# New places for the buffers of a convolution's backward pass (one core, tiles of 128 partitions)

## The chip, the cores and the metric

One core of one Trainium2 chip. The metric is the device time of one execution in microseconds (us). Each kernel below was run several times; I quote the median, and compare only executions whose state was told to be fast, which here is all of them. A run of a kernel also left one execution taken by the hardware profiler: its *profile*. Engines: PE is TensorE (PEld its weight loads), DVE VectorE, ACT ScalarE, POOL GpSimd.

## The reference

The program computes a network of four residual steps and all its gradients:

```python
x = A_q
x = x + A(layernorm(x), k, v, shift_k, ssm_k, ssm_D)   # gated long convolution by FFT
x = x + MLP(layernorm(x), w1, b1, w2, b2)              # gelu
x = x + A(layernorm(x), ...)
x = x + MLP(layernorm(x), ...)
# outputs: x, and the gradients of q, k, v, shift_k, ssm_k (= h), ssm_D, w1, b1, w2, b2
# S = 2048 positions, D = 512 channels, MLP width 1376, bfloat16
# A: k_shift[t] = sum of 4 taps of k times shift_k;  kv = k_shift * v
#    y = causal convolution of kv with ssm_k, + kv * ssm_D;   out = q * y
```

What matters here is the backward pass of A, which comes last: the gradient of kv leads to the gradients of v, k and of the four taps (`shift_k`), and a transform of the spectra gives the gradient of `ssm_k`, called h below.

## The kernel before

The last quarter of the program is `conv_backward`. Its parts, in program order, with cuts marked:

```python
def conv_backward(...):
    dma = nc.gpsimd.dma_start                     # all these loads and stores queue on POOL
    psum = ... "cb_ps" ...                        # "sp": two buffers of PSUM
    gyp = ... "cb_gy" ...                         # GY0..4 (spectra); "Sg": two buffers of 8 KB per partition
    # ... forward transform, products with H and KV, inverse transform into W ... (cut)
    with tc.tile_pool(name="cb_w", side="right", reuse_waits="tile") as wp:
        W = [wp.tile([P, 2, 8, 512], BF16, name=f"Wb{m}") for m in range(2)]
        # ... (cut)
        with tc.tile_pool(name="cb_io", side="right", reuse_waits="tile") as io:
            wdiag = io.tile([P, ND, 4, P], BF16, name="wdiag_b")
            ksbs = [io.tile([P, 4, D], BF16, name="ksb_b", tag="ksb", bufs=4) for i in range(4)]
            # ... loads of wdiag, ks, v (cut)
            gT = io.tile([P, ND, S + 16], BF16, name="gksT")
            nc.vector.memset(gT[:, :, S:S + 16], 0.0)
            for i in range(4):
                for h in range(4):
                    # products on VectorE; four matmuls turn gkv into PSUM tile ps (gt_ps) (cut)
                    if h >= 2:                    # and once more, reversed, into pr (gr_ps)
                        for cc in range(ND):
                            c0 = 256 * (i % 2) + P * (h - 2)
                            nc.scalar.activation(out=W[1][:, cc // 2, 2 * (cc % 2) + i // 2, c0:c0 + P],
                                                 in_=pr[:, 0, cc * P:(cc + 1) * P], func=ACT.Identity)
                    nc.scalar.activation(out=gT[:, :, t0:t0 + P], in_=ps..., func=ACT.Identity)
                yield 3.0
            w0f = W[0][:, :, :, :].rearrange("p e s d -> p (e s d)")
            kcs = [gyp.tile([P, 4096], BF16, name="kTc", tag="Sg", bufs=2)[:, 0:4 * 544] for cc in range(2)]
            kcs += [w0f[:, 2048 + 2176 * x:2048 + 2176 * (x + 1)] for x in range(2)]
            for cc in range(ND):
                dma(out=kcs[cc], in_=dram.kT[:, cc, :, :]...)
            # gradient of k: 256 matmuls gk_ps<-gksT,wdiag, evicted into gk_o (the ksb buffers), stored (cut)
            gwo = io.tile([P, 2, ND, 4], F32, name="gwo", tag="gwo", bufs=1)
            junk = W[0][:, 0, 0:2, :]...
            for cc in range(ND):                  # the shift-filter sums: 4 x 4 x 2 = 32
                for j in range(4):
                    for half in range(2):         # half 0 reads gT, half 1 the reversed copies in W[1]
                        nc.vector.scalar_tensor_tensor(out=junk, in0=g_, scalar=1.0, in1=kc[:, :, k_:k_ + 256],
                                                       op0=ALU.mult, op1=ALU.mult, accum_out=gwo[...])
                    yield 2.2
            gwb = ...; tt(out=gwb, in0=gwo[:, 0], in1=gwo[:, 1], op=ALU.add)
    # cb_io and cb_w end here; the next pool is laid over the same bytes
    with tc.tile_pool(name="cb_gh", side="right", reuse_waits="tile") as hp:      # the h gradient
        tabG = hp.tile([P, 2, 16, NQP], BF16, name="tabG")            # NQP = 272
        # ... two loads of tabG (cut)
        w0 = hp.tile([P, 2, 8, NQP], BF16, name="Wh", tag="Wh", bufs=2)
        th0 = [hp.tile([P, 2, 2, NQP], BF16, name=f"ibh{x}", tag=f"ibh{x}", bufs=3) for x in range(3)]
        gh0 = hp.tile([P, S], BF16, name="gh", tag="gh", bufs=4)
        for cc in range(ND):                      # four channel blocks
            # matmuls gh_ps<-tabG,GY; ScalarE evicts them into Wh (L871); VectorE folds Wh into gh; store (cut)
```

Each `yield N` lets another generator put in some N us of its own work, the weight gradients of the MLP (dw_tp, dw_tm, dw_ps, b1a). Tiles are placed from fixed stacks; a pool opened after another has closed takes the same bytes. `reuse_waits="tile"` means that the first write to a tile waits for all uses of every older tile whose bytes it touches, whole tiles at a time.

## Time and profile before

| | before |
|---|---|
| time, median of 3 executions | 955.77 us (954.72 to 958.27) |
| span of the profiled execution | 952.4 us |
| the changed stage within it: from gksT's memset to b_ps | 782.06 to 947.45 = 165.39 us |

The *stage* is my own measure, used throughout: from the start of VectorE's memset of gksT's pad to the start of b_ps, TensorE's last product. Everything that the change touches lies in it, but for two loads that the changed kernel issues 26.1 and 7.7 us before it. It is worth having because executions differ by some us in work that the change does not touch: over all profiles below the memset falls between 781.7 and 787.2 us, though the program up to there is practically the same, while the stage took 151.00 and 151.01 us in the two profiles of the changed kernel.

The prediction below shows the lines for the wait itself. Beside them, from the page of the kernel before: the span, the granted TensorE clock in 40 slices (tenths of full speed), and the chain that ended last, by engine.

```profile
span 952.4 us, 12919 instructions
...
PEclk9999999978998789869999999979999999997999
...
PE 37%; DVE 30%; ACT 17%; DMA 6%; issue 6%; POOL 3%; SPq 1%; ACTq 0%; DVEq 0%; POOLq 0%
```

Slice 37 of 40 (857 to 881 us) has a clock of 7 amid nines: the gap that the change aims at. VectorE has 30% of the chain, though the page gives TensorE more busy time (83% against 77% of the span). Two stretches around that gap in the kernel before (columns: stretch and length; busy us of PE, PEld, DVE, ACT and POOL with instruction counts; clock; DMA share; GB/s):

```profile
859.00:873.00 14.00, 2.25 (x22) 1.63 (x20) 13.65 (x20) 1.83 (x3) 0.00 (x0) 0.67 0.30 84
873.00:881.00 8.00, 8.00 (x52) 5.96 (x51) 6.94 (x9) 3.89 (x10) 0.78 (x1) 0.73 0.22 66
```

In the first TensorE is busy 2.25 of 14 us. In the second it is busy all the time, at 0.73 of its clock.

### The profile page before, as it was taken

To read this page: it belongs to the slowest core of one execution; us is meant where nothing else is said; L and a number is where in the kernel's file an instruction comes from. 1 tells how busy PE (TensorE), PEld (TensorE's weight loads), DVE (VectorE), ACT (ScalarE), POOL (GpSimd) and SP (SyncE) were. 2 spreads that over 40 slices of the span, in tenths; PEclk is the share of its full clock that TensorE was granted. 3 is DMA by queue.
4 is the path that set the end of the run, shared out by engine and by line. 5 is a ranking of instruction groups with operands and counts; after the bars stand their busy time and mean duration, and the time that the engine had idled before them with its cause. 6 is when DMAs were issued, how large, how long until landed. Compare 5 with 4: busy or idle time off the path is not lost.

```text
span 952.4 us, 12919 instructions
## 1 busy us (share of the span) xinstructions
PE 794.6 (83%) x4754; PEld 406.6 (43%) x4754; DVE 734.0 (77%) x1203; ACT 613.5 (64%) x810; POOL 151.7 (16%) x274
## 2 busy tenths in 40 slices
PE   3698868846786869649999999968999997995998
PEld 2463324422332324214444444434455555853664
DVE  7748489895999979658458878883389995699973
ACT  5867645637997979579835656445665558652664
POOL 5632210021001010100001221220011304200000
PEclk9999999978998789869999999979999999997999
DMA  6568786223445344476798868549076798852331
GB/s 218 173 237 322 280 286 222 90 50 105 138 150 146 130 140 148 139 215 180 249 283 241 246 190 239 166 151 353 2 244 203 266 323 287 288 170 72 118 100 38
DMA packets 157079, 180.87 MB, mean 190 GB/s; under 512 B 50325, under 2 KB 137048, under 8 KB 156504
## 3 DMA queue, kind: packets, MB, share of 16 engines
q1 hardware_dynamic: 142872, 135.70, 46.1%
q0 software_dynamic: 11968, 40.15, 11.7%
q10 hardware_dynamic: 2176, 4.19, 1.2%
q8 instruction: 37, 0.61, 0.3%
q14 instruction: 26, 0.21, 0.1%
HBM read 95.76 MB, written 82.13 MB: 187 GB/s over the span
## 4 chain that ended last, share of the span: by engine, by line
PE 37%; DVE 30%; ACT 17%; DMA 6%; issue 6%; POOL 3%; SPq 1%; ACTq 0%; DVEq 0%; POOLq 0%
PE gn_ps L1134 7%; PE sp_ps L55 7%; PE gh_ps L1116 6%; DVE Wb L55 6%; PE dw_ps L55 6%; ACT g_z L1089 3%; PE gh_ps L55 3%; DVE b1a L55 3%; ACT g_s L1065 3%; ACT g_o L1066 2%; ACT g_q L1062 2%; DVE pr_t L55 2%; DVE pr_u L55 2%; PE z_ps L1087 2%; DMA tabFb<-tabF_d 2%
## 5 line engine op out<-in xcount | busy, mean ns | idle before, releaser
L55 PE MATMUL dw_ps<-G,dw_tm 128*128 128x512 bf16 x704 | 170.8, 381 | 2.2 <-ACT dw_tm L1236 2.2
L1236 ACT ACTIVATE dw_tm<-dw_tp 128x1024 bf16<-128x1024 bf16 x88 | 89.9, 1024 | 68.2 <-PE dw_tp L55 68.2
L1087 PE MATMUL z_ps<-nT_sl,w_sb 128*128 128x512 bf16 x352 | 93.8, 424 | 32.3 <-DMA nT_sl<-n_sl 27.2
L1099 PE MATMUL o_ps<-w_sb,h_sl 128*128 128x512 bf16 x352 | 92.1, 404 | 26.7 <-DVE h_sl L1069 26.4
L55 PEld LDWEIGHTS <-dw_tm 128*128 128x128 bf16 x704 | 64.9, 98 | 62.5 <-ACT dw_tm L1236 2.9
L1118 ACT ACTIVATE gz_sl<-gh_ps 128x512 bf16<-128x512 f32 x88 | 50.2, 594 | 56.5 <-PE gh_ps L1116 53.3
L1134 PE MATMUL gn_ps<-w1T_sb,gz_sl 128*128 128x512 bf16 x352 | 81.4, 379 | 1.3 <-DVE gz_sl L1119 1.3
L1116 PE MATMUL gh_ps<-gT_sl,w2T_sb 128*128 128x512 bf16 x352 | 79.6, 379 | 0.0
L1087 PEld LDWEIGHTS <-w_sb 128*128 128x128 bf16 x352 | 37.3, 107 | 88.4 <-issue 43.0
L1089 ACT ACTIVATE g_z<-z_ps,b1col 128x512 bf16<-128x512 f32 x88 | 55.2, 708 | 27.6 <-PE z_ps L1087 27.6
L1099 PEld LDWEIGHTS <-h_sl 128*128 128x128 bf16 x352 | 35.1, 103 | 79.0 <-DVE h_sl L1069 35.3
L55 PEld LDWEIGHTS <-dw_fm 128*128 128x128 bf16 x704 | 47.8, 100 | 20.9 <-issue 0.8
L55 PE MATMUL dw_tp<-ident,dw_fm 128*128 128x128 bf16 x704 | 54.8, 222 | 0.0
L1134 PEld LDWEIGHTS <-gz_sl 128*128 128x128 bf16 x352 | 34.3, 98 | 43.2 <-DVE gz_sl L1119 2.3
L1116 PEld LDWEIGHTS <-w2T_sb 128*128 128x128 bf16 x352 | 34.4, 98 | 41.1
L55 DVE TENSOR_REDUCE b1a<-dw_fm 128x1 f32<-128x2048 bf16 x22 | 49.6, 2277 | 0.0
L989 POOL TENSOR_SCALAR rstd<-ln_mv 128x4 f32<-128x4 f32 x16 | 7.6, 475 | 248.1 <-DVE ln_mv L987 161.9
L1146 POOL TENSOR_SCALAR bb_diag<-ident,bb_cols 128x128 bf16<-128x128 bf16 x32 | 21.6, 676 | 157.3 <-DVE bb_junk L1143 148.1
L1065 ACT ACTIVATE g_s<-g_t 128x2048 bf16<-128x2048 bf16 (+1 forms) x24 | 42.8, 1784 | 3.6 <-DVE g_t L1064 3.6
L1119 DVE TENSOR_TENSOR gz_sl<-gz_sl,gpb 128x2048 bf16<-128x2048 bf16 (+1 forms) x24 | 27.2, 1134 | 22.7 <-DMA gpb<-gp_d 11.7
L1062 ACT ACTIVATE g_q<-g_z 128x2048 bf16<-128x2048 bf16 (+1 forms) x24 | 43.1, 1798 | 0.1
L1066 ACT ACTIVATE g_o<-g_t 128x2048 bf16<-128x2048 bf16 (+1 forms) x24 | 42.7, 1780 | 0.0
(297 smaller groups left out, 1621.6 us busy)
## 6 DMA issues: line engine op xcount, KB each, us to landing
dw_fm<-h_d SPq DMA_DIRECT2D x22, 512.0 KB, 3.9
dw_fm<-gz_d SPq DMA_DIRECT2D x22, 512.0 KB, 3.8
h_d<-h_sl SPq DMA_DIRECT2D x16, 512.0 KB, 2.9
gp_d<-g_p SPq DMA_DIRECT2D x16, 512.0 KB, 3.3
nb_sl<-n_d SPq DMA_DIRECT2D x16, 512.0 KB, 5.3
gpb<-gp_d SPq DMA_DIRECT2D x16, 512.0 KB, 4.5
gz_d<-gz_sl SPq DMA_DIRECT2D x16, 512.0 KB, 5.2
n_d<-n_sl SPq DMA_DIRECT2D x12, 512.0 KB, 3.3
```

What stands on the lines that cost most here:

```text
L55: return self.tc.keep_in_program_order(f(*args, **kwargs))
L1062: nc.scalar.activation(out=q, in_=zb, func=ACT.Square)
L1065: nc.scalar.activation(out=sg, in_=t, func=ACT.Sigmoid)
L1066: nc.scalar.activation(out=o, in_=t, func=ACT.Sigmoid, scale=-1.0)
L1087: nc.tensor.matmul(ps, lhsT=w.w1[:, dc, c * P:(c + 1) * P], rhs=nT[:, dc, :], start=(dc == 0), stop=(dc == ND - 1))
L1089: nc.scalar.activation(out=zb[:, c - c0, :], in_=ps, func=ACT.Identity, bias=w.b1col[:, c:c + 1])
L1099: nc.tensor.matmul(ps, lhsT=h[:, c, t * P:(t + 1) * P], rhs=w.w2[:, c, :], start=False, stop=(c == NFC - 1))
L1116: nc.tensor.matmul(ps, lhsT=w.w2T[:, dc, c * P:(c + 1) * P], rhs=gT[:, dc, :], start=(dc == 0), stop=(dc == ND - 1))
L1118: nc.scalar.activation(out=gz[:, c, :], in_=ps, func=ACT.Identity)
L1119: nc.vector.tensor_tensor(out=gz[:, c0:c0 + k, :], in0=gz[:, c0:c0 + k, :], in1=gp[:, 0:k, :], op=ALU.mult)
L1134: nc.tensor.matmul(ps, lhsT=gz[:, c, t * P:(t + 1) * P], rhs=w.w1T[:, c, :], start=(c == 0), stop=(c == NFC - 1))
L1236: nc.scalar.activation(out=dst, in_=ps, func=ACT.Identity)
```

## The change

Its intent: the first tiles that the h gradient needs (Wh, tabG) are to lie over memory that the shift-filter sums do not read. The pools of that part share one region of bytes, so this takes two things. What the sums read and lies in W has to leave W: the reversed copies and two of the kT blocks go to `gy_bf`, a tile free by then, and to a small new tile; the junk output goes there too. And the tiles are declared in another order: gksT, the one large tile that the sums read to their end, comes to lie under gh (the tile of the finished h gradient), which VectorE writes only after the sums in any case. As the reversed copies are now contiguous in a way that one instruction can write, four evictions of 128x128 become one of 128x512.

Bytes of each partition, from the programs as built:

| tile | before | after |
|---|---|---|
| gksT (read by the sums) | 81600–98112 | 56768–73280 |
| wdiag, ksb | 61120–81600 | 77760–98240 |
| first Wh | 77600–86304: on gksT | 96160–104864: on the last ksb and W[0] |
| tabG | 60192–77600: on wdiag, ksb | 113568–130976: on W |
| gh, ibh | 95008–130976 | 60192–96160: gh on gksT, ibh on kTc3, wdiag, ksb |

The diff, cut to its core:

```diff
         with tc.tile_pool(name="cb_io", bufs=1, side="right", reuse_waits="tile") as io:
+            gT = io.tile([P, ND, S + 16], BF16, name="gksT")
+            gwo = io.tile([P, 2, ND, 4], F32, name="gwo")
+            kc3 = io.tile([P, 4 * 544], BF16, name="kTc3")
             wdiag = io.tile([P, ND, 4, P], BF16, name="wdiag_b")
... (ksb)
-            gT = io.tile([P, ND, S + 16], BF16, name="gksT")
+            tf = res.gy_bf[:, :, :].rearrange("p t d -> p (t d)")
+            gr = tf[:, 0:4096].rearrange("p (c i q) -> p c i q", c=ND, i=4)
...
-                        for cc in range(ND):
-                            c0 = 256 * (i % 2) + P * (h - 2)
-                            nc.scalar.activation(out=W[1][:, cc // 2, 2 * (cc % 2) + i // 2, c0:c0 + P],
-                                                 in_=pr[:, 0, cc * P:(cc + 1) * P], func=ACT.Identity)
+                        nc.scalar.activation(out=gr[:, :, i, P * (h - 2):P * (h - 1)],
+                                             in_=pr[:, 0, :].rearrange("p (c t) -> p c t", c=ND), func=ACT.Identity)
...
-            kcs += [w0f[:, 2048 + 2176 * x:2048 + 2176 * (x + 1)] for x in range(2)]
+            kcs += [tf[:, 4096:4096 + 2176], kc3]
...
-            gwo = io.tile([P, 2, ND, 4], F32, name="gwo", tag="gwo", bufs=1)
-            junk = W[0][:, 0, 0:2, :].rearrange("p a (b d) -> p (a b) d", b=2)
+            junk = tf[:, 6272:6272 + 1024].rearrange("p (i q) -> p i q", i=4)
... (the sums read gr[:, cc] instead of W[1])
     with tc.tile_pool(name="cb_gh", bufs=1, side="right", reuse_waits="tile") as hp:
+        gh0 = hp.tile([P, S], BF16, name="gh", tag="gh", bufs=4)
+        th0 = [hp.tile([P, 2, 2, NQP], BF16, name=f"ibh{x}", tag=f"ibh{x}", bufs=3) for x in range(3)]
+        w0 = hp.tile([P, 2, 8, NQP], BF16, name="Wh", tag="Wh", bufs=2)
         tabG = hp.tile([P, 2, 16, NQP], BF16, name="tabG")
... (loads of tabG)
-        w0 = hp.tile([P, 2, 8, NQP], BF16, name="Wh", tag="Wh", bufs=2)
-        th0 = [hp.tile([P, 2, 2, NQP], BF16, name=f"ibh{x}", tag=f"ibh{x}", bufs=3) for x in range(3)]
-        gh0 = hp.tile([P, S], BF16, name="gh", tag="gh", bufs=4)
```

More of the change, by code (lines that the diff above doesn't have):

```diff
@@ L804, in conv_backward @@
                                     eng=nc.gpsimd)
-            w0f = W[0][:, :, :, :].rearrange("p e s d -> p (e s d)")
             kcs = [gyp.tile([P, 4096], BF16, name="kTc", tag="Sg", bufs=2)[:, 0:4 * 544] for cc in range(2)]
-            kcs += [w0f[:, 2048 + 2176 * x:2048 + 2176 * (x + 1)] for x in range(2)]
+            kcs += [tf[:, 4096:4096 + 2176], kc3]
             for cc in range(ND):
@@ L830, in conv_backward @@
                         else:
-                            g_ = W[1][:, cc // 2, 2 * (cc % 2):2 * (cc % 2) + 2, :].rearrange("p a (b q) -> p (a b) q", b=2)
+                            g_ = gr[:, cc]
                             k_ = 272 + j
```

## The prediction

> **What bounds the kernel now.** I read the page first, then the chain that ended last, in order of time, for the last quarter; then the waits and the timelines of single engines there. The change touches only this last quarter: the convolution's backward pass, with the MLP's weight gradients (dw_ps, dw_tp, b1a) filled in between. The chain there:
>
> ```profile
> 799.04 0.71 POOL o3B_d L244
> ...
> 802.30 15.68 DMA kTc<-kT_d
> 818.08 1.24 DVE Wb L55 x2
> ...
> 870.88 1.24 DVE Wb L55 x2
> 872.20 0.61 ACT Wh L871
> 872.85 7.65 PE gh_ps L55 x48
> ...
> 942.56 4.98 PE dw_ps L55 x23
> 947.56 0.61 ACT dw_o L1292
> ```
>
> Columns: start, length, engine and tile. From 818 to 873 us VectorE makes the 32 shift-filter sums ("Wb" is their junk output), with a b1a sum in between each few. Then one ScalarE copy of PSUM (Wh) starts, and from there TensorE sets the end. The hand-over is odd, as the h gradient (gh_ps, Wh) takes no data from the sums. The waits from 775 us on name it:
>
> ```profile
> PE gh_ps L55 <- ACT Wh L871: 12.6, 4, 11.8
> ACT Wh L871 <- DVE Wb L55: 11.4, 1, 11.4
> ```
>
> (total us, times, longest.) Each has one long wait. TensorE's timeline shows the place, and beside it the same point of the second channel block, which is undisturbed:
>
> ```profile
> 860.28 0.82 PE L55 MATMUL gh_ps<-tabG,GY 128*128 128x257 bf16 x6
> 872.85 7.65 PE L55 MATMUL gh_ps<-tabG,GY 128*128 128x257 bf16 x48 [11.75 <-ACT Wh L871]
> ...
> 887.42 0.82 PE L55 MATMUL gh_ps<-tabG,GY 128*128 128x257 bf16 x6
> 888.49 5.51 PE L55 MATMUL gh_ps<-tabG,GY 128*128 128x257 bf16 x48 [0.25 <-ACT Wh L871]
> ```
>
> TensorE fills its two PSUM buffers, then idles 11.75 us until ScalarE empties one. The sums wrote no PSUM and no Wh: the wait is one of memory. In the program as built, the first Wh tile has bytes 77600 to 86304 of each partition and gksT 81600 to 98112, so Wh may be written only when the last sum that reads gksT is over (870.88 + 1.22 = 872.1 us, and Wh starts at 872.20). Elsewhere TensorE hardly stands still: from 826 to 860 us it was busy all 34.00 us, from 881 to 948 us for 65.87 of 67. Two things about the idle time matter for its price:
>
> ```profile
> 861.00:872.80 11.80, 0.10 (x1) 0.00 (x0) 11.49 (x18) 0.60 (x2) 0.00 (x0) 0.61 0.27 78
> 872.80:876.00 3.20, 3.15 (x15) 2.21 (x15) 3.20 (x5) 1.09 (x3) 0.04 (x1) 0.50 0.00 0
> 876.00:880.50 4.50, 4.50 (x36) 3.65 (x34) 3.94 (x5) 2.54 (x6) 0.73 (x1) 0.85 0.40 117
> 888.00:894.00 6.00, 5.75 (x52) 4.84 (x50) 5.50 (x6) 4.07 (x9) 0.00 (x0) 1.00 0.54 179
> ```
>
> (stretch and length; busy us of PE, PEld, DVE, ACT, POOL; granted TensorE clock; DMA share; GB/s.) After the idle stretch the clock is 0.50 and then 0.85, later 1.00 again. And VectorE's end:
>
> ```profile
> 936.35 0.17 DVE L55 TENSOR_TENSOR b1o<-b1a 128x11 bf16<-128x11 f32 x1
> 947.71 0.21 DVE L55 COPY b1r<-b_ps 11x128 bf16<-11x128 bf16 x1 [11.19 <-PE b_ps L55]
> ```
>
> VectorE is done 11.19 us before TensorE reaches its last product: that is its slack.
>
> [...]0.50 for the 3.2 us after the gap, 1.00 for 826 to 860 us. So the gap costs more than its length. [...]while Wh waited, nothing behind it ran on ScalarE from 860.80 to 872.20 us, and no weight-gradient matmul filled TensorE's gap. [...]kTc, issued at 802.30 us behind the 1 MB copy of o1B (issued 800.64, 15.9 us to landing, so 816.5), came at 818.0. I use this for when the sums can start.
>
> **The change, part by part.** The order of instructions on TensorE, VectorE and SyncE is unchanged between the two builds, apart from names. ScalarE loses 24 instructions; on the GpSimd queue two of the four kT loads move ahead.
>
> Removed wait: the first Wh tile now has bytes 96160 to 104864, over the last ksb buffer and the start of W[0]. Its first write no longer waits for VectorE, only for its matmuls and for the second gk_o store (issued 819.76 us; the median landing is 8.5 us, so about 829). tabG now lies over W, free when the last gr_ps matmul is done (808 us). gksT's place goes to the gh tiles, which VectorE writes after the sums anyway. TensorE's wait then shrinks from 11.75 to the 0.25 us of the other blocks: **11.5 us**.
>
> Removed cold clock: the 48 matmuls took 7.65 us here and 5.51 us in block two: **2.1 us**. [...]both terms move the end in full.
>
> ScalarE's reversed copies: 8 times four copies (about 0.280 us each alone, 0.78 us as a group of four in the timeline) become 8 single ones of 128x512. I price those as the gksT copies of that size, 0.598 us. TensorE waits for the first of each pair (0.29 us four times in the timeline), so some 0.14 us shorter four times: **0.6 us**. The second copy of each pair ends before anything waits.
>
> Unchanged: the 32 sums (1.22 us each, also with junk and operand in gy_bf), all matmuls, the tail behind TensorE's last product (947.5 to 952.4 us). The kT loads for blocks three and four go out after ksb instead of at 806 us, but the sums start with block one, which still needs the buffers of vb and stands behind o1B in the queue. I leave the sums at 818 to 873 us.
>
> Sum: 11.5 + 2.1 + 0.6 = 14.2 us, so a span of 938.2 us, and 955.8 - 14.2 = **941.6 us** (1.5% less).
>
> Does VectorE have room? After the sums and two b1a (877.8 us) it works a block and its b1a in turn. In these blocks it waited 1.17, 1.10, 1.08, 1.29 and 2.15 us for Wh, together 6.8; with TensorE ahead these go. Then b1o comes at 936.4 - 6.8 = 929.6 us, TensorE's last product at 947.5 - 14.2 = 933.3: 3.7 us of slack left. Block three of gh needs the first Wh buffer again: ScalarE at 901.3 - 14.2 = 887.1 us, VectorE finished with it at 886.9 - 1.2 = 885.7. Close, 1.4 us. The dw_fm loads wait for b1a of four units earlier: the nearest, released at 877.8 us, lands at 882 and is wanted past 890.
>
> **The rivals.** (a) VectorE becomes the bound. For: only 3.7 us and 1.4 us are left, and a later start of the sums shifts all of it. Against: the five waits that go. If its times stayed as they were (b1o at 936.4), the end would come 3 us later than I say: 945 us. (b) The moved loads disturb. For: the gy_bf load can start at about 774 us, when its memory is free, and from 775 to 786 us the DMA share was 1.06 at 363 GB/s with the reloads of G. 544 KB at that rate is 1.5 us, which could hold TensorE at G or push the stores, o1B and kTc behind it: 943 us, up to 945 together with (a). (c) A new memory wait takes the old one's place, of Wh for a store or of tabG for W. Against: those are free at 829 and 808 us, 30 us before use; I see no such wait in the build. It would give back most: 950 to 956 us. (d) Less DMA behind 806 us lets kTc land earlier and the sums start sooner. That only adds to VectorE's slack and leaves 941 us; to pass 2% (936.7 us), TensorE would have to lose 5 us more, nearly all its waiting of 786 to 811 us (25.00 - 19.76 = 5.2 us), which nothing here touches.
>
> **Range and chances.** The first two terms are one gap and its cold clock, read off directly, so their error is below 1 us. (a) and (b) can take 1 to 4 us; the three runs of before lie within 3.6 us. So 937.5 to 946.5 us. Over 2% faster needs 19.1 us: 0.05. Slower by 2% has no mechanism: 0.01. Within 2%: 0.94.
>
> **What would show it.** Right: no wait of Wh for VectorE; the first 48 gh_ps matmuls in about 5.5 us with the clock at 1.00 between 860 and 880 us; TensorE's last product near 933 us; VectorE's wait for it down from 11.2 to about 4 us; the reversed copies at 0.6 us each, eight of them. Wrong: a new wait over 2 us of gh_ps for Wh in block three or four, or of dw_ps for G near 780 us (a, b); b1o after 933 us (a); or an eviction that waits for a store (c).

## The result, and the profile after

The changed kernel takes **942.22 us** (median of four, 940.49 to 943.36) against 955.44 us (four: the three above and one more; 954.72 to 958.27), with a ratio of 0.9855 [0.9829, 0.988]. That is 1.5% less, within the 2% that count as the same. Ratios and intervals here and below come with each run's result and are worked out from the fast executions, so they are not quite the ratio of the medians that I quote. The result was correct, and all executions were fast.

The profile after, the same three lines of its page:

```profile
span 940.2 us, 12816 instructions
...
PEclk9998998977999779878999999989999999999999
...
PE 52%; ACT 18%; DVE 15%; issue 6%; DMA 5%; POOL 3%; SPq 1%; ACTq 0%; POOLq 0%; DVEq 0%
```

The dip of the clock in slice 37 is gone, and the 32 sums (with the b1a between them), which had been on the chain from 818 to 872 us, are not on it any more. That VectorE's share of the chain fell as far as from 30% to 15% is only in part due to this: followed back from its new end, the chain also takes another way through the work before 800 us, which is practically the same in both kernels (from 700 to 800 us VectorE has 84 us of it before and none after, TensorE 9 and 95 us). The chain in order of time shows TensorE in their place, in the profile after (start, length, engine and tile):

```profile
858.67 1.94 PE dw_ps L55 x9
...
861.50 0.56 PE gh_ps L55 x5
862.08 0.61 ACT Wh L871
862.74 5.50 PE gh_ps L55 x48
```

The same two stretches in the profile after; this execution ran 2.1 us later at the memset, which does not matter for stretches of this length:

```profile
859.00:873.00 14.00, 13.64 (x111) 9.70 (x112) 13.76 (x19) 8.92 (x16) 0.00 (x0) 1.00 0.30 85
873.00:881.00 8.00, 7.69 (x67) 6.09 (x66) 7.87 (x10) 5.56 (x12) 0.78 (x1) 1.00 0.23 72
```

TensorE is busy 13.64 us instead of 2.25, at full clock in both. TensorE's timeline and the waits of the stage after the change:

```profile
862.74 5.50 PE L55 MATMUL gh_ps<-tabG,GY 128*128 128x257 bf16 x48 [0.25 <-ACT Wh L871]
```

```profile
DVE gy_bf L55 <- DMA kTc<-kT_d: 18.8, 1, 18.8
...
ACT Wh L871 <- PE gh_ps L55: 4.9, 14, 0.6
DVE b1r L55 <- PE b_ps L55: 4.1, 1, 4.1
...
PE gh_ps L55 <- ACT Wh L871: 1.1, 4, 0.3
```

The wait of 11.75 us is now 0.25, like the other three blocks. For Wh, ScalarE now waits only for the matmuls that it evicts (at most 0.6 us each), and not for VectorE. The first line is the wait of the sums for their first kT block, as long as before (18.9 there): nothing is changed in when the sums start, only in who waits for them. (Before, the junk output lay in Wb, so the sums were listed under Wb; now they are under gy_bf.) VectorE's end, after:

```profile
931.16 0.17 DVE L55 TENSOR_TENSOR b1o<-b1a 128x11 bf16<-128x11 f32 x1
935.46 0.21 DVE L55 COPY b1r<-b_ps 11x128 bf16<-11x128 bf16 x1 [4.13 <-PE b_ps L55]
```

Its slack fell from 11.19 to 4.13 us. The reversed copies, by tile, before and after (count; shortest, median and longest duration in ns):

```profile
L794 ACT ACTIVATE Wb<-gr_ps x32: 271/280/300, 788.4 to 808.9; 128x128 bf16<-128x128 f32 x32
```

```profile
L796 ACT ACTIVATE gy_bf<-gr_ps x8: 592/592/594, 790.5 to 809.8; 128x512 bf16<-128x512 f32 x8
```

The whole stage, cut at the starts of TensorE's first products of each kind:

| part | before | after | difference | predicted |
|---|---|---|---|---|
| memset to the first gk_ps | 29.45 | 28.70 | −0.75 | −0.6 |
| gk_ps to the first gh_ps | 48.44 | 48.43 | −0.01 | 0 |
| gh_ps block one to block two | 27.14 | 13.49 | −13.65 | −11.5 − 2.1 = −13.6 |
| block two to b_ps | 60.36 | 60.38 | +0.02 | 0 |
| stage | 165.39 | 151.00 | −14.39 | −14.2 |

Spans differ by only 12.2 us because this execution after was 2.14 us later at the memset.

### The profile page after: what moved, and what is told of

The parts are those of the page before. It is cut to its first block, busy times and chain, and to the rows that moved or that the text cites. A ratio compares the mean times of both kernels' runs of the same rounds, so it can differ in the third digit from the quotient of the medians.

```text
span 940.2 us, 12816 instructions
## 1 busy us (share of the span) xinstructions
PE 792.6 (84%) x4674; PEld 406.8 (43%) x4754; DVE 733.6 (78%) x1203; ACT 612.1 (65%) x786; POOL 151.4 (16%) x274
## 4 chain that ended last, share of the span: by engine, by line
PE 52%; ACT 18%; DVE 15%; issue 6%; DMA 5%; POOL 3%; SPq 1%; ACTq 0%; POOLq 0%; DVEq 0%
PE dw_ps L55 14%; PE gn_ps L1134 7%; PE gh_ps L1116 7%; PE sp_ps L55 6%; PE iv_ps L55 4%; PE dw_tp L55 4%; ACT g_z L1089 3%; PE gh_ps L55 3%; ACT g_s L1065 3%; ACT g_o L1066 3%; ACT g_q L1062 2%; PE z_ps L1087 2%; DMA tabFb<-tabF_d 2%; DMA nT_sl<-n_sl 2%; ACT n_sl L1009 2%
## 5 line engine op out<-in xcount | busy, mean ns | idle before, releaser
L55 PE MATMUL dw_ps<-G,dw_tm 128*128 128x512 bf16 x673 | 165.3, 380 | 5.1 <-ACT dw_tm L1236 3.5
L1069 DVE TENSOR_TENSOR h_sl<-g_s,g_z 128x2048 bf16<-128x2048 bf16 (+1 forms) x24 | 27.1, 1130 | 20.4 <-ACT g_s L1065 20.4
```

Of the source, the lines that this page charges most:

```text
L55: return self.tc.keep_in_program_order(f(*args, **kwargs))
```

## The experiments

Theory A: the gain is the place of the first Wh tile off gksT, with a place of tabG off what the sums read as its condition; it is worth the length of the gap plus the cold clock behind it, and TensorE is the only bound of the stage afterwards. Rivals: B, the evictions or the moved loads bring the gain; C, VectorE has become the bound or nearly so. "Stage" is as defined above (165.39 before, 151.00 after), from each run's profile. All twelve kernels gave correct results, and all executions were fast. They ran in three calls on two chips (`warm_gap2`, `four_copies`, `swap_kT` and `swap_fine` on one, the others on another), each in rounds with the kernel before, whose medians were 955.95, 955.93 and 955.74 us there.

### 1. Wh back on gksT, all else as after

```diff
+        w0 = hp.tile([P, 2, 8, NQP], BF16, name="Wh", tag="Wh", bufs=2)
         gh0 = hp.tile(...)
         th0 = ...
-        w0 = hp.tile([P, 2, 8, NQP], BF16, name="Wh", tag="Wh", bufs=2)
         tabG = hp.tile(...)
```

Wh now lies at 60192–77600, over gksT.

> The changed kernel with one thing put back: the tiles of the last stage in another order, so that the two Wh tiles lie over gksT again and wait for the last sum that reads it, while tabG, the evacuated buffers and the single reversed copies stay as changed. My theory (the gain is one memory wait of Wh and the cold clock behind it): Wh waits for VectorE about 11 us again, the 48 gh_ps matmuls take about 7.6 us, time 954.7 us (before less the 0.7 us of the copies). Rival (the gain comes from the evacuation of W or from the earlier kT loads): it keeps most of the 13 us, 942 to 945 us.

956.19 us, ratio to before 1.0001 [0.9991, 1.0012]; stage 164.78. The wait came back with its old length, and so did the cold clock behind it (0.50 over the next 3.50 us). TensorE's timeline and ScalarE's wait in this kernel:

```profile
876.57 7.30 PE L55 MATMUL gh_ps<-tabG,GY 128*128 128x257 bf16 x48 [12.23 <-ACT Wh L871]
```

```profile
ACT Wh L871 <- DVE gy_bf L55: 11.9, 1, 11.9
```

This kernel has the single evictions, the moved loads and the evacuated W, and gains nothing measurable in the total (0.61 us in the stage). So the place of Wh carries the gain, and B is out as its main cause.

### 2. and 3. Each half of the change alone

`evac_only` is the kernel after with the old order of the last pool, so that tabG lies over gksT:

```diff
-        gh0 = hp.tile(...); th0 = ...; w0 = hp.tile(... name="Wh" ...)
         tabG = hp.tile([P, 2, 16, NQP], BF16, name="tabG")
+        w0 = hp.tile(... name="Wh" ...); th0 = ...; gh0 = hp.tile(...)
```

> The evacuation alone: W is freed, gksT and the fourth kT buffer come first in their pool, but the last stage keeps its old order of tiles, so that tabG lies over gksT. My theory: the load of tabG now waits for the sums (about 875 us) and lands near 886 us, TensorE stands some 26 us before gh_ps and restarts cold, 970 us (965 to 974): slower than before, so the evacuation brings nothing without the new order. Rival (evacuation alone is the gain): 942 us.

`order_only` is the kernel before with gksT and gwo declared first and the new order of the last pool, while the copies, kT blocks and junk stay in W, over which tabG then lies:

```diff
         with tc.tile_pool(name="cb_io", ...) as io:
+            gT = io.tile([P, ND, S + 16], BF16, name="gksT")
+            gwo = io.tile([P, 2, ND, 4], F32, name="gwo")
...
+        gh0 = hp.tile(...); th0 = ...; w0 = hp.tile(... name="Wh" ...)
         tabG = hp.tile([P, 2, 16, NQP], BF16, name="tabG")
-        w0 = hp.tile(...); th0 = ...; gh0 = hp.tile(...)
```

> The order alone, in the kernel before: gksT first in its pool and the last stage in its new order, but junk, two kT buffers and the reversed copies still in W. My theory: tabG and Wh lie over W, which the sums read and write to the end (873 us), so tabG lands near 884 us, TensorE stands some 24 us, 968 us (963 to 972). Rival (the new order alone is the gain): 942 us.

970.41 us, ratio 1.0153 [1.0131, 1.0174], and 970.3 us, ratio 1.0148 [1.0128, 1.0167]; stages 179.78 and 179.44. TensorE's first gh_ps products in `evac_only`, then in `order_only`:

```profile
885.03 0.61 PE L55 MATMUL gh_ps<-tabG,GY 128*128 128x257 bf16 x2 [24.29 <-DMA tabG<-tabG_d]
```

```profile
882.57 0.61 PE L55 MATMUL gh_ps<-tabG,GY 128*128 128x257 bf16 x2 [20.53 <-DMA tabG<-tabG_d]
```

Now the table itself must wait for the sums, and a transfer on top: in `evac_only` its two loads went out at 877.8 and 879.0 us, and TensorE started at 885.0. The two products behind the gap took 0.61 us in both kernels, against 0.38 us for two of the same form in their second blocks. The stage is 14 us longer than before, where TensorE waited 11.75. Either half alone makes the kernel 1.5% slower, which is within the 2% that count as the same but clear of the noise; only both together free Wh and tabG at once. The two halves of this change do not add up.

### 4. and 5. The gap kept, its cold clock taken away

The kernel before with needless 128x128 matmuls inside the gap, into a part of the PSUM tile that nothing reads, meant to hold TensorE's clock at 1.00 though the products behind it wait as long: 180 in `warm_gap`, 215 in `warm_gap2`.

```diff
+                    if cc == 0 and k1 == 4:
+                        for x in range(180):          # warm_gap2: 215
+                            nc.tensor.matmul(ps[:, 1, 384:512], lhsT=consts.ident, rhs=consts.ident, start=True,
+                                             stop=True)
                     if slot == sr:
```

> The kernel before with its wait untouched, but 180 matmuls of 128x128 whose result nobody reads (about 10 us) put into TensorE's idle time before the third gh_ps group, in unused columns of the PSUM tile. My theory (2.1 us of the gain are the cold clock): the clock stays near 1.00 there, the 48 matmuls take about 5.5 us instead of 7.65, time 953.3 us. Rival (the 48 matmuls are slow for another reason, say they wait for ScalarE's copies, and clock recovers by itself): they stay above 7 us and the time at 955.4 us or more.

954.95 us, ratio 0.9987 [0.9969, 1.0006]; stage 166.03. I had put in too few: 2.97 us of the gap were left, and the clock fell all the same (1.00 in the gap, 0.73 over the next 2.90 us and 0.79 over the 4.30 us after those). The products after it in `warm_gap`:

```profile
879.17 7.14 PE L55 MATMUL gh_ps<-tabG,GY 128*128 128x257 bf16 x48 [2.97 <-ACT Wh L875]
```

Inconclusive, so once more with 215.

> As warm_gap, with 215 needless matmuls (about 12.2 us) for 180: there 2.97 us of the wait stayed empty and the 48 matmuls still took 7.14 us. Cold-clock theory: with at most some 1 us left empty, the clock stays at 1.00 and the 48 matmuls take about 5.5 us; time 2 us below before, 953.5 us. Rival (slow for another reason): still above 7 us.

955.7 us, ratio 0.9998 [0.9982, 1.0013]; stage 164.77. The added matmuls and the products after them:

```profile
863.07 12.17 PE L55 MATMUL gh_ps<-ident 128*128 128x128 bf16 x215
...
876.30 5.50 PE L55 MATMUL gh_ps<-tabG,GY 128*128 128x257 bf16 x48 [1.06 <-ACT Wh L875]
```

In the trace the prediction's second term is confirmed: with a gap of 1.06 us the 48 products take 5.50 us at clock 1.00 instead of 7.65, and from the start of the first Wh to b_ps it is 73.35 us instead of 75.25. The time did not fall, so my expectation of the total was wrong. Part of it is in the trace: the first sum starts 37.3 us after the memset instead of 36.0, and everything that waits for the sums with it: −1.9 + 1.3 = −0.6, and the stage has −0.62, which is too small for the total to show. `warm_gap` shows the same late start (37.2). The sums begin long before the added matmuls run. The delay is in the queue of the loads: the copy of o1B, which stands before the first kT block, went out 18.6 us after the memset in the kernel before and in both of these, but took 17.2 us to land in `warm_gap2` and 17.1 in `warm_gap`, against 15.9 before and 15.6 to 16.2 in every other profile; the first sum started 1.5 us after it had landed in the kernel before and in both of these. Why it took longer stays open.

### 6. The kernel after once more

> The changed kernel again, as a yardstick on the same chip for the other runs of this call: 942 us, between 940.5 and 943.5.

942.35 us, ratio 0.9857 [0.984, 0.9873]; stage 151.01, against 151.00 in the first profile.

### 7. and 8. More work for VectorE behind the sums

The kernel after with 4 (`dve_plus3`) or 12 (`dve_plus8`) needless products behind the last sum:

```diff
+            for _ in range(4):                        # dve_plus8: 12
+                tt(out=junk, in0=gr[:, 0], in1=gr[:, 1], op=ALU.mult)
             gwb = gyp.tile([P, ND, 4], BF16, name="gwb", tag="gwb", bufs=1)
```

The prediction saw two margins of VectorE: 3.7 us at its end, and 1.4 us at the Wh buffer that block three needs again.

> The changed kernel with four needless products of 128x1024 (about 0.69 us each, 2.8 us in all) on VectorE right behind the last sum. Theory A (VectorE's nearest margin is the first Wh tile, which ScalarE fills again for block three at 889.06 us while VectorE is done with it at 887.45): TensorE loses about 1.2 us in block three, 943.4 us, and TensorE's last product still finds VectorE ready. Theory B (only the 4.1 us at the end count): no change, 942.2 us.

> The same with twelve products, 8.3 us. Theory A: gh_ps of block three waits about 6.7 us for Wh, and as that is long enough for a cold clock some 1 to 2 us come on top: 949 to 951 us. Theory B (only the 4.1 us at the end count): 8.3 - 4.1 = 4.2 us, 946.4 us.

`dve_plus8`: 952.46 us, ratio 0.9956 [0.994, 0.9971]; stage 160.62. `dve_plus3`: 946.16 us (944.2 to 947.38), ratio 0.9892 [0.9876, 0.9909]; stage 152.47. Block three in `dve_plus8`, then in `dve_plus3`:

```profile
895.38 7.76 PE L55 MATMUL gh_ps<-tabG,GY 128*128 128x257 bf16 x48 [7.62 <-ACT Wh L873]
```

```profile
893.05 5.51 PE L55 MATMUL gh_ps<-tabG,GY 128*128 128x257 bf16 x48 [1.73 <-ACT Wh L873]
```

The place is the one foretold, the Wh buffer of block three. With 12 products the wait is 7.37 us over the usual 0.25 and the cold clock (0.50 over the next 3.62 us) 2.25 us over 5.51: 9.62, and the stage has +9.61. With 4 (2.86 us in the trace) the wait is 1.48 us over the usual and the clock stays full (1.00); the stage has +1.46. So C is not true of the kernel after, but nearly: the small margin is real, and its overrun cost what it was long, with 12 products also the 2.25 us of the clock.

One thing does not fit: `dve_plus3`'s median is 3.8 us over the kernel after of the same call, where its stage explains 1.5. Its profiled execution was 2.84 us later at the memset already, before anything that the edit touches; this is the slowest of its four executions, and the lateness is the larger part of what it is slower by. The other executions leave no trace that would tell whether they were late there too, or lost the clock at block three. Open.

### 9. The old four evictions

The kernel after with four evictions of 128x128 again, into the new place:

```diff
-                        nc.scalar.activation(out=gr[:, :, i, P * (h - 2):P * (h - 1)], in_=pr[:, 0, :]..., func=ACT.Identity)
+                        for cc in range(ND):
+                            nc.scalar.activation(out=gr[:, cc, i, P * (h - 2):P * (h - 1)],
+                                                 in_=pr[:, 0, cc * P:(cc + 1) * P], func=ACT.Identity)
```

> The changed kernel with the one part put back that is no memory: the reversed copies again in four pieces of 128x128. Theory: TensorE's four waits of 0.29 us for them return, the stretch from gksT's memset to gk_ps grows by 0.6 to 0.8 us (28.7 in the changed kernel), time 943.0 us against 942.3. Rival (no effect): below 0.2 us in the trace.

942.85 us, ratio 0.9872 [0.9846, 0.9898]; stage 151.73, +0.73. Four waits of TensorE of 0.29 us for these copies are back; each sets the next product 0.68 us behind the one before instead of 0.49, so 4 x 0.19 = 0.76. That is the −0.75 of the first row of the table above, alone, and it is too small for the total to show.

### 10. The weight-gradient work in smaller portions

With TensorE the bound, what is left is its waiting between 786 and 811 us (busy 20.35 of 25 us in the kernel after), where products, ScalarE's copies and the loads take turns. The kernel after with the filling work handed in by slice of `h` and not by `i`:

```diff
                     nc.scalar.activation(out=gT[:, :, t0:t0 + P], ...)
-                yield 3.0
+                    yield 0.75
```

> A try at a better version: the changed kernel, but the weight-gradient matmuls that fill TensorE between the convolution's steps are let in after each of the four h steps of a slice (0.75 each) and not after all four (3.0). Theory: TensorE's waits for the gksT copies (3.6 us in eight pieces between 786 and 811 us) are filled, gain 2 to 3 us, 939.7 us. Rival: ScalarE bounds that stage, its copies of the transposes only push the gksT copies back, and nothing is gained (942 us).

942.52 us, ratio 0.9855 [0.9834, 0.9876]; stage 151.91. From the memset to gk_ps it is 24.44 us instead of 28.70: 4.3 us gained. They are lost again in two places, in TensorE's timeline of `fine_fill`:

```profile
859.58 0.62 PE L55 MATMUL dw_tp<-ident,dw_fm 128*128 128x128 bf16 x8 [1.62 <-DMA dw_fm<-gz_d]
...
890.60 7.14 PE L55 MATMUL gh_ps<-tabG,GY 128*128 128x257 bf16 x48 [2.00 <-ACT Wh L871]
```

TensorE arrives earlier while VectorE does not: 1.62 us of waiting for a load whose buffer VectorE (b1a) frees, 1.75 us over the usual in block three, and 1.64 us of cold clock behind that. This adds up to 5.0, against the 4.3 gained, and the stage has +0.91. The margins of experiments 7 and 8 are used up from the other side. The stretch just behind that gap (columns as before):

```profile
890.60:894.00 3.40, 3.40 (x17) 2.44 (x17) 3.40 (x2) 1.04 (x2) 0.10 (x1) 0.53 0.62 192
```

### 11. and 12. VectorE earlier, alone and with smaller portions

The sums wait for a kT block whose buffer is that of vb and whose load stands behind a large copy (o1B; in the kernel before it was issued at 800.64 us and took 15.9 us to land, and the first sum started 1.5 us later). In the kernel after there are two other kT blocks that are loaded early. `swap_kT` gives those to channel blocks one and two:

```diff
-            kcs += [tf[:, 4096:4096 + 2176], kc3]
+            kcs = [tf[:, 4096:4096 + 2176], kc3] + kcs
```

`swap_fine` is that with the edit of experiment 10.

> The changed kernel with the kT buffers in another order: the two that load early serve the first two blocks of the sums, the two that stand behind o1B in the queue the last two. The sums then start when gksT is complete, near 811 us, and not at 820. Theory (TensorE is the bound, VectorE's start moves only its slack): same time, 942.3 us, and VectorE's wait for b_ps grows from 4 to 10 us or more. Rival (VectorE's start still bounds the end): 3 us or more are gained.

> A try at a better version: swap_kT together with fine_fill. In fine_fill alone TensorE reached gk_ps 4.3 us sooner after gksT's memset, but lost it to a dw_fm wait (1.62 us) and to Wh in block three (2.00 us, with a cold clock behind it), both because VectorE had not come along. Theory: with the sums 9 us earlier both waits go and the 4 us stay: 938.3 us (937 to 939.5). Rival (a load of dw_fm or the queue takes it back): 941 to 942.5 us.

`swap_kT`: 942.03 us, ratio 0.9866 [0.9837, 0.9895]; stage 150.96. Its first sum of the trace:

```profile
808.07 1.22 DVE L55 SCALAR_TENSOR_TENSOR gy_bf<-gksT,gy_bf 128x1024 bf16<-128x1024 bf16 x1 [6.91 <-ACT gksT L799]
```

Twelve us earlier than after, and VectorE is done 11.18 us before TensorE's last product instead of 4.13. The time is the same: TensorE alone bounds the kernel after, and C falls.

`swap_fine`: **937.4 us** (935.23 to 939.31), ratio 0.9811 [0.9787, 0.9835]; stage 146.75, 4.25 us less than after. Block three and VectorE's last wait in `swap_fine`:

```profile
883.01 5.51 PE L55 MATMUL gh_ps<-tabG,GY 128*128 128x257 bf16 x48 [0.25 <-ACT Wh L871]
...
928.75 0.21 DVE L55 COPY b1r<-b_ps 11x128 bf16<-11x128 bf16 x1 [11.18 <-PE b_ps L55]
```

With VectorE early, the 4.25 us from the memset to gk_ps (24.45 instead of 28.70) reach the end. Neither edit gains anything alone, and together they beat both kernels. By the interval it cannot be said whether this is over or under 2% against the kernel before.

## All profiles in one table

Waits of TensorE for Wh and the 48 products behind them are those of the longest wait of each profile.

| kernel | median us | stage us | longest wait for Wh | 48 products |
|---|---|---|---|---|
| before | 955.44 | 165.39 | 11.75 | 7.65 |
| after / again | 942.22 / 942.35 | 151.00 / 151.01 | 0.3 | 5.5 |
| wh_on_gksT | 956.19 | 164.78 | 12.23 | 7.30 |
| evac_only | 970.41 | 179.78 | 0.3 (24.29 and 2.48 for tabG) | – |
| order_only | 970.3 | 179.44 | 0.3 (20.53 and 4.79 for tabG) | – |
| warm_gap | 954.95 | 166.03 | 2.97 | 7.14 |
| warm_gap2 | 955.7 | 164.77 | 1.06 | 5.50 |
| four_copies | 942.85 | 151.73 | 0.3 | 5.5 |
| dve_plus3 | 946.16 | 152.47 | 1.73 | 5.51 |
| dve_plus8 | 952.46 | 160.62 | 7.62 | 7.76 |
| fine_fill | 942.52 | 151.91 | 2.00 | 7.14 |
| swap_kT | 942.03 | 150.96 | 0.3 | 5.5 |
| swap_fine | 937.4 | 146.75 | 0.3 | 5.51 |

## Why the prediction was right

The prediction was 941.6 us, in a range of 937.5 to 946.5, and within 2%; the median is 942.22 us. Its steps in turn:

- **The removed wait, 11.5 us.** Right: 11.75 to 0.25 us. Experiment 1 brings it back by the place of Wh alone.
- **The removed cold clock, 2.1 us.** Right: 7.65 to 5.50 us. That both terms would move the end in full was my estimate; they make 13.6, and the part from block one to block two lost 13.65. Experiment 5 takes the clock away without the gap and confirms the term in the trace, though not in the total. That a gap of this kind is followed by the low clock was shown from both sides, by `dve_plus8` too: 0.50 after 11.75 us (before) and after 7.62 us (`dve_plus8`), 1.00 after 1.06 us (`warm_gap2`).
- **The single copies, 0.6 us.** Right in kind and a little small: 0.75 in the profile, and 0.73 by itself in experiment 9. The prediction has TensorE's wait for each pair 0.14 us shorter; it went altogether, which was worth 0.19 us each. The price of one copy, taken from the gksT copies (0.598), was measured at 0.592.
- **The sums unmoved.** Right: the first kT block came 36.0 us after the memset in both profiles, so rival (d), an earlier start of the sums, did not happen.
- **VectorE's room.** Foreseen at the end: 3.7 us; measured: 4.13. The five waits that were to go were worth 6.8 us; from the memset to b1o it is 146.96 us instead of 154.29, so 7.3. At the Wh buffer of block three: 1.4 foreseen, and VectorE finished with it at 887.45 us, where ScalarE wrote it at 889.06: 1.6. Experiment 7 measures the same margin: 2.86 us were added to VectorE and the wait grew by 1.48, so 1.4 were free. Rival (a) named the right place, but the kernel after stays within its margin.
- **The moved loads, rival (b).** A little: of the loads issued from 14.2 us before the memset to 43.8 us after it, the eight reloads of G took a median of 7.4 us to land instead of 6.2 (6.7 in the repeat), the eight dw_fm loads 8.8 instead of 8.7. TensorE waited for none of them.
- **A new memory wait, rival (c).** None in the kernel after. Experiments 2 and 3 show that the risk was real: either half of the change alone runs into one, of over 20 us.
- **The total.** The stage lost 14.39 us against 14.2 foreseen. The span is 940.2 us, not 938.2, because this execution was 2.14 us later at the memset than the profiled one before. Such differences are in the spread of each kernel's executions, and in the range given. The medians differ by 13.2 us; that the predicted total lies within 0.6 us of the measured one is in part luck, and the parts of the stage say more.

## What to carry to other kernels

Where an engine waits for another that gave it no data, look at the bytes: a tile laid over one that is still being read waits for the last reader (Wh here started 0.1 us after the last sum that read gksT), and where the waiting engine sets the end, as TensorE here, moving the tile was worth the wait plus the cold clock behind it (11.50 and 2.15 us here). Check every tile that the freed stage needs first, not only the one that is named in the wait, for half of such a move can be worse than none (14 us of stage more here). And once the wait is gone, measure the margin of the engine that used to be waited for, as it decides whether the next gain reaches the end.

## What the runs show beyond the prediction, and what they leave open

- After short gaps TensorE's clock fell too. After 2.00 us (`fine_fill`, with TensorE busy at clock 1.00 for the 3.4 us before the gap) the clock was 0.53 for the next 3.4 us and the 48 products took 7.14 us; after 2.97 us (`warm_gap`) 7.14 us too. After 1.06 (`warm_gap2`) and 1.73 us (`dve_plus3`) they took 5.50 and 5.51, as without a gap. Each is one profile. The price hardly depended on the length of the gap beyond that: 1.6 to 2.3 us here (7.14 to 7.76 us for the products after gaps of 2.00 to 12.23 us, against 5.5).
- A single gap can come from memory: 11.75 us once, gone with nearly the same memory (kTc3 adds 4 KB per partition) in another order. What the gap waited for was an engine that gave no data, as VectorE gave none to Wh here.
- Why the copy of o1B landed 1.2 to 1.3 us later in `warm_gap` and `warm_gap2` than in the kernel before, and the first sum 1.1 to 1.3 us later with it, and why executions of nearly the same program differ by up to 5.5 us (781.7 to 787.2) before the stage begins: the runs show it and do not settle it.
